# Turning 32x32 blocks on VectorE and through HBM instead of 128x128 tiles on TensorE, in a sketched-attention and token-mixing kernel

## The chip, the cores and the metric

The kernel runs on one core of a Trainium2 chip. A core has five engines that work through queues of their own and wait for each other by semaphores: TensorE (PE in the profile, with its weight loads as PEld), VectorE (DVE), ScalarE (ACT), GpSimd (POOL) and SyncE (SP, which here only issues transfers). The metric is the device time of one execution in microseconds, lower is better.

## The reference

For four batches of 1088 tokens, polynomial attention with four heads of 32 columns and features of 8 x 8, and a token mixer on its output, all in float32:

```python
def phi(x):                                   # x: (4, 4 heads, 1088, 32)
    a = einsum('rd,bhsd->bhsr', S1, x)        # r = 8
    b = einsum('rd,bhsd->bhsr', S2, x)
    return einsum('bhsi,bhsj->bhsij', a, b).reshape(..., 64)
kv  = einsum('bhsf,bhsd->bhfd', phi(k), v)
z   = phi(k).sum(axis=2)
num = einsum('bhsf,bhfd->bhsd', phi(q), kv)
den = einsum('bhsf,bhf->bhs', phi(q), z)[..., None] + 1e-06
x   = (num / den) as (4, 1088, 128)

theta = x @ w_theta
y = einsum('ts,bsd->btd', w_tok_r, x * cos(theta)) + einsum('ts,bsd->btd', w_tok_i, x * sin(theta))
u = x + y
out = u + max(u @ w_ch, 0)
```

## The kernel before

Tokens are cut into 9 chunks of 128 and handled in 3 groups of 3 chunks. The kernel does not call the engines in the order of its text: every step is recorded as an operation with its engine, its buffers and its predecessors (`op`, `buf`), and at the end the operations are issued in the order of the long string `ORDER`, with the buffer of each tile taken from the string `PLACES`. Both strings were found ahead of time by an annealing search with a planned duration for each operation (the second argument of `op`, and `fly` for a transfer). `SPINS` names operations ahead of which TensorE does some products of an idle tile. Each engine works through its own operations in this order, so an instruction that has to wait holds up all that stand behind it on its engine.

Stages, by batch `b` and group `g`:

- `load`: k, q, v by SP; `row`: the 17 rows of the token weights, 128 x 1088 in 64 bits each, loaded by SP and made into float32 by two ScalarE and two VectorE instructions a row (L564, L566, and L305 and L301 on VectorE).
- `kT`, `kf`, `kv`, `sums`, `rest`, `chain`, `kvb`: features of k, their products with v and the scales of the denominator; chains of small VectorE instructions. Batches 2 and 3 share one chain.
- `qT`, `q0`, `levels`, `den`: q turned and cut into two parts (in batches 2 and 3 the second part comes from an accumulating transfer of the POOL queue), its features by products on TensorE, and the denominators by ten VectorE instructions of a batch.
- `num` (`outputs_x`, L995): for each group VectorE makes the products of q's features, 128 tokens x 768 (3 chunks x 4 heads x 64). TensorE turns them in six 128x128 tiles (`trs`, L1019: two times three, against the identity) into two banks, ScalarE copies each bank to the tile `qT` (L1023), and two products with `bd` (k's features times v) give x, turned, which ScalarE copies to `xT` (L1032).
- `theta`: x times w_theta on TensorE; x itself turned back to tokens by three 128x128 turns (`turn`, L1052) into a bank; cosine and sine on ScalarE; VectorE multiplies the turned x with both into `z`. In batch 3, x is first scaled by a power of two (`xs`, L1044).
- `mix` for batches 0 and 1: the 17 weight rows, each times z of the batch, 512-column banks summed up over the rows; batch 0 goes through all three groups of a row at a time. Batches 2 and 3 are mixed together by seven products of half size (`winograd`), for which VectorE makes sums of weight rows (`ac`) and differences of z (`zc`).
- `out`: the last product with w_ch. The result lies turned; VectorE turns 32x32 blocks (`V.transpose`, L1161), and four stores (two on SP, two on ScalarE's queue for batches 2 and 3), one for each 32 columns, put the blocks where they belong, in runs of 32 numbers.

So a 128x128 turn on TensorE is one matmul against the identity and needs a copy out of its bank, while a VectorE turn stays within 32x32 blocks and leaves it to a transfer to put the blocks in order.

Of the kernel before, what the change touches and what calls it, by code (L numbers as in the profile page):

```python
# [29 lines left out]
    "6 4 2 5 44 0 1 47 342 3 45 7 50 8 347 49 9 10 11 58 12 29 48 13 76 83 14 46 70 64 15 84 86 16 133 87 77 85 71 "  # L30
    "26 17 139 146 30 89 88 19 72 140 78 73 343 147 74 90 21 18 149 134 27 345 79 91 94 25 150 20 40 80 92 65 32 93 "
    "31 344 41 95 99 127 148 100 43 66 157 151 337 135 22 102 158 101 67 96 128 303 42 68 103 97 348 311 35 28 104 "
    "313 105 36 304 159 305 106 315 160 350 136 108 307 161 306 107 137 109 308 59 23 129 110 314 309 24 111 316 "
    "237 61 112 312 195 33 113 98 130 231 37 238 114 225 115 131 232 152 244 34 69 116 310 233 60 239 226 75 117 "
    "196 123 118 38 81 349 119 120 122 121 346 422 234 357 240 82 424 338 351 53 352 426 425 317 423 153 340 427 "
    "339 428 154 39 429 382 62 124 155 430 141 208 156 125 431 245 201 162 432 126 189 202 197 163 190 433 165 164 "
    "198 318 358 166 191 227 63 434 209 142 359 167 203 435 132 168 436 138 228 367 204 192 169 56 437 171 170 372 "
    "354 438 172 362 143 439 441 173 452 442 174 144 440 353 175 443 51 210 176 445 453 145 444 455 178 446 177 246 "
    "456 179 448 360 447 459 449 180 341 460 461 450 454 181 462 457 182 186 463 183 185 187 184 451 361 521 464 "
    "465 519 355 522 458 466 523 520 356 467 524 468 469 484 525 369 526 527 368 485 470 528 471 377 473 188 57 529 "  # L40
    "472 486 364 530 474 220 531 487 532 363 533 221 374 534 488 392 535 373 542 538 536 549 539 543 537 545 211 "
    "544 550 212 552 546 540 553 247 551 222 215 547 541 213 365 554 548 214 248 475 555 366 556 251 572 558 477 "
    "557 559 574 489 370 560 478 561 575 479 371 564 562 480 476 216 566 563 54 481 252 567 217 249 568 199 569 581 "
    "250 378 483 604 482 605 576 375 570 565 582 218 571 577 606 379 376 573 607 578 387 583 384 579 584 580 253 "
    "393 193 235 223 194 254 224 219 394 255 261 200 265 383 262 608 397 266 205 609 268 267 264 380 585 263 610 "
    "385 206 395 269 323 207 270 389 396 611 586 324 271 321 381 319 587 320 273 588 388 272 274 241 627 322 628 "
    "275 407 390 276 490 412 229 398 831 629 386 277 589 278 399 400 279 630 631 401 402 408 590 612 280 281 632 "
    "297 391 491 835 414 832 492 409 283 410 282 413 411 417 493 403 284 415 291 404 405 494 325 406 495 292 416 "
    "419 496 285 326 286 418 833 327 287 288 290 497 420 293 421 498 289 296 52 834 294 499 500 654 501 507 652 655 "
    "508 650 653 502 298 651 633 256 656 328 634 657 513 332 299 591 658 514 635 659 257 592 660 330 661 636 662 "  # L50
    "593 258 594 55 663 259 331 595 664 333 637 665 596 666 597 673 503 598 329 638 674 334 676 669 335 667 504 639 "
    "677 336 295 505 675 230 300 236 599 668 242 670 680 678 260 243 671 679 681 672 640 688 613 687 683 641 689 "
    "684 695 690 614 691 693 714 692 682 712 694 715 697 716 713 698 301 717 685 699 718 600 686 719 515 720 703 "
    "601 696 705 721 642 700 789 302 701 706 790 516 707 704 702 791 709 780 708 722 615 781 723 616 724 711 808 "
    "517 792 710 518 809 725 617 618 726 619 506 727 810 742 643 620 735 743 728 745 782 744 793 746 838 644 736 "
    "749 621 783 737 738 622 731 729 784 645 730 747 732 739 733 740 734 811 741 798 748 799 750 800 762 751 753 "
    "764 801 765 755 785 752 756 794 766 757 623 768 754 624 758 771 836 812 773 802 759 774 813 770 760 803 761 "
    "795 775 828 763 776 772 767 848 839 777 769 840 841 837 849 778 804 829 850 860 786 851 779 842 886 843 862 "
    "787 852 857 926 830 625 646 788 853 861 796 854 858 868 855 844 856 845 859 864 814 869 797 805 863 877 865 "
    "846 647 878 889 879 870 927 871 887 904 847 880 890 881 930 872 866 806 602 894 867 882 603 883 888 873 928 "  # L60
    "874 967 815 626 807 875 932 905 884 934 509 876 895 892 818 648 896 931 906 933 907 939 929 897 937 940 891 "
    "816 885 941 510 908 935 948 909 936 949 893 898 950 938 924 819 942 910 911 943 951 899 912 952 913 944 925 "
    "953 817 945 820 954 822 821 946 900 649 947 901 968 902 955 903 970 956 957 511 980 958 512 823 971 824 981 "
    "825 982 972 983 826 919 984 920 973 969 974 959 990 961 991 975 921 976 922 923 914 992 960 915 977 916 978 "
    "917 962 979 985 964 963 827 1000 986 918 1001 987 993 965 994 988 1002 966 995 989 996 1004 997 1003 998 1005 "
    "1006 999 1007 1010 1008 1011 1012 1009 1013 1014 "
)
PLACES = (
    "3 1 9 1 1 11 1 21 2 13 15 7 1 9 1 16 6 19 4 0 5 6 0 3 6 3 4 4 1 1 11 3 2 5 6 8 2 1 0 2 4 6 5 2 2 0 7 8 0 1 7 3 "
    "5 5 2 9 6 1 0 4 6 5 7 4 2 1 12 1 7 4 2 0 0 2 0 1 8 4 4 4 3 19 2 5 4 6 14 0 6 0 5 1 7 4 11 1 2 7 8 0 0 7 1 7 21 "  # L70
    "4 0 3 3 7 5 6 1 2 2 6 3 10 12 3 2 2 3 5 8 14 3 4 4 1 4 1 2 2 0 0 6 3 2 2 9 10 5 0 4 0 0 5 21 7 10 7 6 11 3 6 1 "
    "3 0 7 7 11 1 6 4 7 2 6 7 9 5 1 0 4 4 6 7 2 3 7 0 0 2 6 5 3 0 2 3 2 0 12 2 6 8 3 11 10 0 7 18 3 17 5 1 20 17 3 "
    "16 0 4 9 11 3 2 13 2 9 15 3 19 20 1 4 1 1 9 16 1 9 2 3 9 19 2 4 4 3 9 0 7 1 2 11 4 6 0 0 3 5 3 6 0 4 3 4 4 2 2 "
    "5 2 5 6 7 3 3 1 2 7 0 3 6 5 4 3 3 0 2 2 3 5 3 1 0 4 3 2 5 9 7 4 0 4 7 0 2 2 1 2 1 1 3 0 0 7 7 1 3 2 7 2 0 7 7 "
    "4 1 4 1 3 2 3 5 0 0 5 0 1 0 6 3 7 14 6 6 0 3 1 6 5 3 4 3 1 7 1 0 2 4 7 6 1 3 0 6 5 4 5 4 2 0 6 3 4 21 1 21 1 4 "
    "2 5 2 6 2 3 6 4 4 1 1 6 5 0 4 4 3 1 0 0 4 0 6 6 0 1 7 1 4 5 7 14 2 3 0 4 6 2 5 0 2 3 2 6 4 5 4 2 1 6 3 3 2 4 7 "
    "1 5 "
)
SPINS = (
    "76:2 139:4 158:1 109:1 166:1 172:5 174:1 1010:1 "  # L80
# [15 lines left out]
QDMA = (False, False, True, True)  # L96
UDMA = (True, True, False, False)
# [124 lines left out]
def dve2(n):  # L222
    return (n / 2 + 150) / 960.0
# [11 lines left out]
def kernel(  # L235
# [49 lines left out]
    pools = {c: maker(c, w) for c, (_, w) in classes.items()}  # L285
    L = Layout(classes)
# [30 lines left out]
    def vop(n, fn, w, r, two=False, lk=0):  # L317
        op("V", dve2(n) if two else dve(n), fn, w, r, lk=1 if two else lk)

# [675 lines left out]
    def outputs_x(b, lv, pool_qp):  # L995
# [3 lines left out]
        for g in range(NG):  # L999
# [13 lines left out]
            qT = buf("g3", (2, GW), F32, "qT")  # L1013
            for n in range(2):
                tr = buf("ps", (GW,), F32, "qptr")

                def trs(n=n, tr=tr, qp=qp):
                    for i in range(GC):
                        T.transpose(tr()[:, i * P:(i + 1) * P],  # L1019
                                    qp()[:, i * H + 2 * n:i * H + 2 * n + 2].rearrange("p h i j -> p (h i j)"), ident())  # L1020

                op("P", 0.33, trs, [tr], [qp])
                op("A", act(GW), lambda n=n, tr=tr, qT=qT: A.copy(qT()[:, n], tr()), [(qT, n)], [tr])  # L1023
            xp = buf("ps", (GW,), F32, "xp")

            def num(xp=xp, qT=qT):
                for n in range(2):
                    mm(xp()[n * 64:(n + 1) * 64], bd()[:, 2 * n:2 * n + 2].rearrange("p h d -> p (h d)"), qT()[:, n],
                       True, True)
# [7 lines left out]
        for g in range(NG):  # L1037
            at("theta", b, "_", g)
            x = buf("ps", (GC, P), F32, "x")
# [10 lines left out]
            def turn(x=x, xs=xs, off=off):  # L1050
                for i in range(GC):
                    T.transpose(x()[:, i], xs()[:, off + i * P:off + (i + 1) * P], ident())  # L1052

            def theta(g=g, th=th):
                for i in range(GC):
                    y_ = xt()[:, g * GW + i * P:g * GW + (i + 1) * P]
                    mm(th()[:, i], y_, w2()[:, 0], True, True)

            op("P", 0.67, theta, [th], cells(xt, g * GW, (g + 1) * GW) + [w2])
            op("P", 0.33, turn, [x], dep)  # L1060
            op("A", act(GW), lambda cs=cs, th=th: A.activation(cs()[:, 0], th(), AF.Copy, bias=ROUND), [(cs, 0)], [th])  # L1061
            vop(GW, lambda cs=cs, th=th: stt(cs()[:, 1], cs()[:, 0], ROUND, th(), ALU.subtract, ALU.subtract), [(cs, 1)],
                [th, (cs, 0)])
# [303 lines left out]
```

## Time and profile before

| | |
|---|---|
| three runs | 222.06, 221.21, 222.2 us, median 222.06 |
| the profiled execution | 222.07 us, its span 220.3 us |
| granted TensorE clock | 0.997 |
| VectorE busy | 173.8 us (79%) in 395 instructions |
| ScalarE busy | 117.0 us (53%) in 228 |
| transfers | 23195 packets, 34.68 MB; 17028 of them under 512 bytes |

Each group line of the profile reads: line, engine, operation, out<-in by the program's names, partitions x elements, count | busy us in all, mean ns of one | idle time just before, and what ended it. Most helpers record all their operations in one line (L301 for two-operand VectorE work, L321 for TensorE products), so lines are told apart by tiles and shapes. Busy times of neighbours on an engine overlap a little, since the next instruction starts before the one ahead has drained; the time from start to start is shorter than the busy time.

### The profile page before, as it was taken

How to read it: one execution, taken by the hardware profiler on the slowest of the kernel's cores; microseconds unless marked ns; L12 is line 12 of the kernel's file. 1: busy time of each engine (PE TensorE's matmuls, PEld its weight loads, DVE VectorE, ACT ScalarE, POOL GpSimd, SP SyncE). 2: the span in 40 equal slices, each digit the busy share in tenths (PEclk: the TensorE clock that was granted, in tenths of full speed). 3: DMA queues.
4: the chain of work that ended last, by engine and by line, in shares of the span. 5: the costliest groups of instructions: out<-in, count | busy, mean ns of one | idle time of the engine just before them, and what ended most of it. 6: DMA issues, size and time to landing. Idle time of an engine off the chain costs nothing.

```text
span 220.3 us, 5088 instructions
## 1 busy us (share of the span) xinstructions
PE 213.3 (97%) x2052; PEld 160.9 (73%) x2052; DVE 173.8 (79%) x395; ACT 117.0 (53%) x228; POOL 22.6 (10%) x44
## 2 busy tenths in 40 slices
PE   7999998999999999999999999999999999999993
PEld 3787897776678576766667668777688888788872
DVE  4699999999989998998906862899268899955661
ACT  3799998789978985675324355633484000000000
POOL 2356000000050110000222040000200000000000
PEclk9999999999999999999999999999999999999998
DMA  5999099993979863775435342003400002102373
GB/s 166 413 417 402 22 332 391 360 413 86 343 228 244 221 240 152 288 318 204 98 119 88 122 110 39 1 11 54 68 0 0 3 0 46 26 0 43 53 102 76
DMA packets 23195, 34.68 MB, mean 157 GB/s; under 512 B 17028, under 2 KB 18308, under 8 KB 20996
## 3 DMA queue, kind: packets, MB, share of 16 engines
q1 hardware_dynamic: 17908, 29.28, 37.9%
q0 software_dynamic: 1728, 4.65, 9.9%
q10 hardware_dynamic: 3536, 0.43, 1.3%
q8 instruction: 16, 0.26, 0.5%
q14 instruction: 7, 0.06, 0.1%
HBM read 27.48 MB, written 2.23 MB: 135 GB/s over the span
## 4 chain that ended last, share of the span: by engine, by line
PE 85%; DVE 8%; ACT 2%; issue 2%; DMA 1%; POOL 1%; POOLq 0%
PE ps L321 75%; PE ps L1019 4%; PE ps L359 3%; DVE big L301 2%; PE ps L1052 2%; DVE g L301 1%; PE ps L927 1%; DMA out<-g 1%; DVE lv L301 1%; PE ps L703 1%; DVE hf L305 1%; DVE sm L308 1%; ACT big L614 1%; ACT g L706 1%; DVE big L305 0%
## 5 line engine op out<-in xcount | busy, mean ns | idle before, releaser
L321 PE MATMUL ps<-big,zs 128*128 128x384 f32 (+4 forms) x398 | 111.6, 423 | 0.4 <-DVE big L301 0.4
L321 PEld LDWEIGHTS ps<-big,zs 128*128 128x128 f32 x398 | 71.2, 190 | 26.7 <-issue 0.8
L1151 ACT COPY g<-ps 128x128 f32<-128x128 f32 (+1 forms) x3 | 0.9, 301 | 48.1 <-PE ps L1143 47.8
L566 ACT ACTIVATE big<-zs 128x1088 int32<-128x1088 uint32 (+1 forms) x18 | 21.1, 1177 | 4.9 <-DVE big L301 3.2
L301 DVE CUSTOM_DVE_ANT_0 big<-big,big 128x2176 uint16<-128x2176 uint16 x17 | 21.8, 1285 | 0.4 <-ACT big L566 0.4
L321 PE MATMUL ps<-big,big 128*64 128x64 f32 (+2 forms) x208 | 21.7, 276 | 0.0
L564 ACT ACTIVATE big<-zs 128x1088 f32<-128x1088 f32 x17 | 20.7, 1217 | 0.8 <-DMA zs<-w_tok 0.7
L321 PEld LDWEIGHTS ps<-big,big 128*64 128x64 f32 (+1 forms) x208 | 16.7, 154 | 3.0 <-issue 0.5
L301 DVE TENSOR_TENSOR big<-big,big 128x544 f32<-128x544 f32 x24 | 16.7, 716 | 0.1
L1023 ACT COPY g<-ps 128x384 f32<-128x384 f32 x24 | 10.4, 485 | 11.1 <-PE ps L1019 10.1
L301 DVE TENSOR_TENSOR zs<-ps,g 128x768 f32<-128x768 f32 (+2 forms) x20 | 12.5, 629 | 2.9 <-ACT g L1065 2.6
L315 POOL DMA_DIRECT2D big<-hf x6 | 5.9, 986 | 81.6 <-DVE sm L305 40.3
L305 DVE TENSOR_SCALAR big<-big 128x1088 int32<-128x1088 int32 x17 | 12.2, 721 | 0.6 <-ACT big L564 0.6
L301 DVE TENSOR_TENSOR g<-lv 128x768 f32<-128x768 f32 x12 | 11.0, 954 | 0.6 <-PE ps L321 0.5
L321 PEld LDWEIGHTS ps<-w,big 128*128 128x128 f32 x80 | 10.3, 192 | 1.6 <-issue 0.6
L308 DVE SCALAR_TENSOR_TENSOR g<-g,ps 128x384 f32<-128x384 f32 x12 | 6.5, 550 | 5.9 <-ACT g L1061 5.7
L321 PE MATMUL ps<-w,big 128*128 128x128 f32 x80 | 11.1, 277 | 0.0
L1019 PEld LDWEIGHTS ps<-ident,g 128*128 128x128 f32 x72 | 8.2, 141 | 2.3 <-issue 0.8
L1061 ACT ACTIVATE g<-ps 128x384 f32<-128x384 f32 x12 | 5.7, 490 | 7.9 <-PE ps L321 5.3
L359 PE MATMUL ps<-idle 128*128 128x384 bf16 x27 | 8.0, 414 | 1.9 <-POOL idle L361 1.3
L1019 PE MATMUL ps<-ident,g 128*128 128x128 f32 x72 | 9.5, 275 | 0.0
L308 DVE SCALAR_TENSOR_TENSOR big<-ps,even,big 128x256 f32<-128x256 f32 (+1 forms) x10 | 4.8, 497 | 5.7 <-PE ps L321 5.7
(185 smaller groups left out, 339.6 us busy)
## 6 DMA issues: line engine op xcount, KB each, us to landing
zs<-w_tok SPq DMA_DIRECT2D x17, 1088.0 KB, 7.0
big<-k_l SPq DMA_DIRECT2D x6, 576.0 KB, 6.0
big<-hf POOLq DMA_DIRECT2D x6, 576.0 KB, 5.1
big<-q_l SPq DMA_DIRECT2D x4, 576.0 KB, 9.4
big<-v_l SPq DMA_DIRECT2D x4, 576.0 KB, 10.8
g<-big POOLq DMA_DIRECT2D x4, 192.0 KB, 3.8
out<-g SPq DMA_DIRECT2D x16, 48.0 KB, 1.9
g<-big POOLq DMA_DIRECT2D x2, 160.0 KB, 3.2
```

The source lines that it names most:

```text
L301: eng.tensor_tensor(out=o, in0=a, in1=b, op=f)
L305: (eng or V).tensor_scalar(out=o, in0=a, scalar1=s1, scalar2=s2, op0=op0, **kw)
L308: (eng or V).scalar_tensor_tensor(out=o, in0=a, scalar=s, in1=b, op0=op0, op1=op1)
L315: op("G", 0.9, lambda: G.dma_start(dst(), src(), accum_op=ALU.add), w, r, fly=fly)
L321: T.matmul(o, lhs, rhs, start=start, stop=stop, skip_group_check=True)
L359: T.matmul(nowhere() if home is None else view(home, (GW,), F32), idle()[:, 0:P], idle(), start=True, stop=True, skip_group_check=True)
L564: op("A", 0.22 + n * 0.0009, lambda: A.activation(dfn(), words_of(raw(), n)[1].bitcast(F32), AF.Prelu, scale=2.0**-112, alpha=-(2.0**32)), ...
L566: op("A", 0.22 + n * 0.0009, lambda: A.activation(stp(), words_of(raw(), n)[0].bitcast(U32), AF.Copy, scale=2.0**-29), [stp], [raw])
L1019: T.transpose(tr()[:, i * P:(i + 1) * P], qp()[:, i * H + 2 * n:i * H + 2 * n + 2].rearrange("p h i j -> p (h i j)"), ident())
L1023: op("A", act(GW), lambda n=n, tr=tr, qT=qT: A.copy(qT()[:, n], tr()), [(qT, n)], [tr])
L1052: T.transpose(x()[:, i], xs()[:, off + i * P:off + (i + 1) * P], ident())
L1061: op("A", act(GW), lambda cs=cs, th=th: A.activation(cs()[:, 0], th(), AF.Copy, bias=ROUND), [(cs, 0)], [th])
```

## The change

Two lists, `NFAR` and `XFAR`, say for which batches a turn is made in the new way: the products of q's features of batches 2 and 3, and x of batch 2. In these, a new helper `turned` records three operations in place of TensorE's turns: one VectorE transpose of all 32x32 blocks (768 columns for a group of q, 384 for one of x), four writes to a scratch tensor in HBM, one for each 32 partitions, that put the blocks at their turned places in runs of 32 numbers, and one plain read back into the tile. The writes and the read are on SP's queue, and the read waits until the four writes have landed. For q this replaces six TensorE turns and two ScalarE copies; for x it replaces three turns, and the tile `x` now lies in the memory on the chip rather than in a bank. The product `num` reads its operand by chunk with a step, because the two head pairs lie side by side. The order, the buffers and the idle products (`SPINS`) were searched for anew, starting from the order before.

```diff
-    "6 4 2 5 44 0 1 47 342 3 45 7 50 8 347 49 9 10 11 58 12 29 48 13 76 83 14 46 70 64 15 84 86 16 133 87 77 85 71 "
+    "6 4 2 5 44 0 1 45 58 3 47 7 50 8 342 48 11 9 46 12 347 13 76 83 14 49 64 337 15 77 84 86 65 10 87 16 29 94 17 "
...
 SPINS = (
-    "76:2 139:4 158:1 109:1 166:1 172:5 174:1 1010:1 "
+    "76:2 15:2 84:2 89:6 135:1 189:1 166:3 439:2 521:1 1005:1 "
 )
...
+NFAR = (False, False, True, True)
+XFAR = (False, False, True, False)
...
+    far = ctx.enter_context(tc.tile_pool(name="far", bufs=1, space=bass.MemoryType.DRAM))
...
+    def turned(cls, dst, src, r, n, name):
+        blocks = buf(cls, (n,), F32, "tb")
+        vop(n, lambda: V.transpose(out=blocks(), in_=src()), [blocks], r)
+        there = Buf(None, (n,), F32, name)
+        there.ap = far.tile([P, n], F32, tag=name, name=name)
+        nf = P // SQ
+
+        def scatter():
+            for f in range(nf):
+                SY.dma_start(there().rearrange("(a i) (x b j) -> b i x a j", a=nf, b=nf, j=SQ)[f],
+                             blocks()[f * SQ:(f + 1) * SQ].rearrange("i (x a j) -> i x a j", a=nf, j=SQ))
+
+        op("S", 0.0, scatter, [there], [blocks], lk=nf, fly=1.8, n=n * nf)
+        op("S", 0.1, lambda: SY.dma_start(dst(), there()), [dst], [there], lk=1, fly=4.6)
...
+            if NFAR[b]:
+                qT = buf("g3", (GC * 2 * P,), F32, "qT")
+                turned("g3", qT, lambda qp=qp: qp().rearrange("p n i j -> p (n i j)"), [qp], GC * 2 * P, f"fq{b}{g}")
+                qTn = lambda n, qT=qT: qT().rearrange("p (c n t) -> p n c t", n=2, t=P)[:, n]
+            else:
...
+                qTn = lambda n, qT=qT: qT()[:, n].rearrange("p (c t) -> p c t", t=P)
...
-                    mm(xp()[n * 64:(n + 1) * 64], bd()[:, 2 * n:2 * n + 2].rearrange("p h d -> p (h d)"), qT()[:, n],
-                       True, True)
+                    mm(xp()[n * 64:(n + 1) * 64].rearrange("m (c t) -> m c t", t=P),
+                       bd()[:, 2 * n:2 * n + 2].rearrange("p h d -> p (h d)"), qTn(n), True, True)
...
-            x = buf("ps", (GC, P), F32, "x")
+            x = buf("g1", (GC * P,), F32, "x") if XFAR[b] else buf("ps", (GC * P,), F32, "x")
...
-            op("P", 0.33, turn, [x], dep)
+            if XFAR[b]:
+                turned("g1", x, lambda xs=xs, off=off: xs()[:, off:off + GW], dep, GW, f"fx{b}{g}")
+            else:
+                op("P", 0.33, turn, [x], dep)
```

## The prediction

> **What bounds the kernel now.** I read the page first, then the chain of waits in order of time, the windows, the groups by shape and the transfers. A span of 220.3 us lies in an execution of 222.07 us; the median of the three runs shown is 222.06 us, so sums made against this execution hold for the median as they stand. A change under 0.5% (1.1 us) can't be told from none.
>
> The first two parts of the page and the chain in order of time (start, length, what):
>
> ```profile
> PE 213.3 (97%) x2052; PEld 160.9 (73%) x2052; DVE 173.8 (79%) x395; ACT 117.0 (53%) x228; POOL 22.6 (10%) x44
> ```
>
> ```profile
> 34.88 0.34 PE ps L359
> ...
> 66.23 0.33 PE ps L1052 x3
> ...
> 126.87 1.31 PE ps L1019 x12
> ...
> 216.84 0.29 DVE g L308
> ```
>
> From 34.88 us to the last product the chain is TensorE's own queue, one instruction behind the other. A turn there costs 0.33/3 or 1.31/12, both 0.109 us. But "TensorE is the bound" is only half of it. The windows (busy time and count of PE, PEld, DVE, ACT, POOL; clock; DMA share; GB/s):
>
> ```profile
> 35.00:60.00 25.00, 24.96 (x309) 18.14 (x309) 24.66 (x56) 22.52 (x39) 0.00 (x0) 1.00 0.81 310
> 60.00:85.00 25.00, 24.88 (x313) 17.65 (x312) 22.91 (x45) 20.08 (x41) 4.48 (x5) 1.00 0.82 246
> 85.00:110.00 25.00, 25.00 (x93) 16.16 (x92) 23.60 (x48) 15.04 (x17) 1.29 (x1) 1.00 0.56 200
> 110.00:130.00 20.00, 20.00 (x235) 14.28 (x235) 11.14 (x25) 7.92 (x17) 4.10 (x6) 1.00 0.38 94
> 130.00:150.00 20.00, 20.00 (x181) 14.78 (x178) 12.68 (x26) 9.59 (x22) 0.77 (x2) 1.00 0.23 47
> ```
>
> Up to 110 us VectorE is as full as TensorE (24.66 of 25, 22.91, 23.60); after it, it is little over half full. A shorter TensorE queue pays only where VectorE can deliver sooner.
>
> **What leaves and what comes.** The groups by shape (busy us, mean ns | idle before):
>
> ```profile
> L1019 PE MATMUL ps<-ident,g 128*128 128x128 f32 x72 | 9.5, 275 | 0.0
> ...
> L1023 ACT COPY g<-ps 128x384 f32<-128x384 f32 x24 | 10.4, 485 | 11.1 <-PE ps L1019 10.1 <-ACT g L1023 0.8 <-PE ps L321 0.2
> ...
> L1161 DVE STREAM_TRANSPOSE g<-g 128x384 f32<-128x384 f32 x4 | 2.3, 572 | 0.0
> ...
> L1161 DVE STREAM_TRANSPOSE g<-big 128x256 f32<-128x256 f32 x2 | 0.9, 445 | 1.4 <-DMA out<-g 1.4
> ```
>
> TensorE loses half of the 72 turns of q (batches 2 and 3: 36) and the 9 turns of x of batch 2: 45 x 0.109 = 4.9 us, all from the chain. ScalarE loses 12 of 24 copies (12 x 0.485 = 5.8 us), after 110 us, where it is under half full: nothing. Five more idle products (32 for 27, 0.18 us each by the chain's five in 0.92 us) stand nearly all ahead of 35 us, where TensorE waits: nothing, 0.9 us if all were on the path. VectorE gains six turns of 768 columns, which no row shows. From 256 to 384 columns the rows rise by 127 ns, 0.99 ns a column, so 768 cost 0.572 + 384 x 0.00099 = 0.95 us; bounds are two of 384 (1.14) and the 128x768 product of VectorE (0.95). Three of 384 columns come on top. Consecutive VectorE instructions overlap by about 0.09 us, so start to start it is 6 x 0.87 + 3 x 0.48 = 6.7 us more. The product with x reads the same number of columns from the same number of rows, from on-chip memory rather than TensorE's banks; the row 128x768 costs 0.954 us either way (g<-lv and zs<-ps,g).
>
> **The HBM trip.** Transfers (KB each, median us to landing):
>
> ```profile
> q10 hardware_dynamic: 3536, 0.43, 1.3%
> ...
> out<-g SPq DMA_DIRECT2D x16, 48.0 KB, 1.9
> ```
>
> 1.3% of 16 engines' 220.3 us over 3536 packets is 13 ns for a packet of at most 128 bytes. A trip of q writes 3072 such packets: 3072 x 13 / 16 = 2.5 us of all engines, spread over four issues that the store rows show 0.48 us apart. So: issues 1.9, landing of the last 1.9 (stores: 1.5 to 3.3), read issue 0.35. No row has a 384 KB read on a free queue; the nearest is the 576 KB v load issued at 122.20, whose packets ran from 123.17 to 125.63, 3.4 us. I take 3.0, between the 2.7 of the 128 KB store and 3.4; crowded q loads took up to 11.7. A trip costs about 7.1 us for q and, with half the bytes, 6.4 for x.
>
> The built order shows what covers it. I walked each engine's new order and added start-to-start times of the rows. From the end of the first turn of x to the product that needs it, VectorE has 9.5 us of other work (the rest of batch 3's denominators, q products, one weight sum), and TensorE needs that product 0.6 us later. For q of batch 2 the cover is 13.9 us, for batch 3 some 15. All 45 new issues stand behind the last weight load and the last v load in SP's queue, so no load waits for them; one group's output store waits behind a read, which no one waits for. SP does hold later writes behind a read that waits for its own write: the reads of q of batch 3 stand behind all three writes, which leaves about 3 us of their 15. On POOL's queue the accumulating transfer of batch 3's q shares the engines with the trips: VectorE releases it 10.3 us before TensorE needs it, against 1.0 us of issue, 4.2 of landing and 3.5 of a trip's engine time (2.5 for the writes, 1.0 for the read at the v load's 188 ns a packet). The trips cost nothing, then; without the cover each would cost its 7.1 us.
>
> [...]
>
> **The new bound.** Here the order matters. Work up to the same places, start to start, in us:
>
> ```
> place (what TensorE waits for)          before: PE  DVE  trace DVE/PE    after: PE  DVE
> levels of batch 1 (chain of batch 1)           38.7 42.0  46.4 / 46.6          37.7 42.0
> first product with weight row 6                79.5 64.0  69.5 / 88.8          64.7 70.8
> k times v of batch 2                           69.6 72.5  78.4 / 78.7          68.8 73.8
> first product with weight row 16              102.8 100.2 108.8 / 112.1        91.0 96.0
> ```
>
> Before, VectorE had 8.7 us of idle time by row 16 (108.8 less 100.2) and TensorE 9.3; VectorE was 2.6 us of work ahead there. After, it is 5.0 us behind: the anneal puts row 16 11.8 us earlier in TensorE's work but only 4.2 earlier in VectorE's. So at row 16 VectorE sets the time: 96.0 plus its idle time. Bounds: 4.4 (what it had by 46.4 us, if it never waits again) and 8.7 (all of before's). A VectorE that is later waits less for others, but it waits in order and ScalarE's releases come close too; I take the middle, 6.5. TensorE then passes row 16 at 96.0 + 6.5 + 0.2 (semaphore, from the 46.4/46.6) = 102.7. Left are 201.2 - 91.0 = 110.2 us of its work (total 201.2, was 206.1) and the 1.2 us that it lost after row 16 before (10.5 at the end less 9.3): 214.1, against 216.6 before. The tail of one copy, one addition and one store is the same. Sum: -4.9 from the turns, +2.4 from the new waits, -2.5 us: 219.6 us. Behind row 16 the leads are smaller than before (the Winograd product that waits for the first difference of z: VectorE 21.7 us of work ahead before, 14.1 after), yet the waits that VectorE must make for batch 2's and 3's levels and for the last group of q leave this about even with TensorE; I hold 1 us for it in the range.
>
> **Rivals.** *TensorE alone is the bound:* VectorE waits at most 4.4 us by row 16. The full fill of 35 to 60 us speaks for it, the growing idle time of VectorE after 60 us against. 222.07 - 4.9 + 0.3 = 217.5 us.
> *VectorE waits as before* (8.7 us by row 16): TensorE ends at 216.3, 221.8 us, no change to be measured. For it: VectorE's waits after 60 us were for ScalarE and TensorE, and ScalarE's queue stays full there (22.52 and 20.08 of 25).
> *The trip is late:* the product with x sits in VectorE's order, and what is queued behind it are all further z, their sums and TensorE's next products. Beyond 9.5 + 0.6 = 10.1 us each us of the x trip is one on the path. With the slow ends of the rows (issues of 1.97, landing 3.3, a crowded read of 11.7) a trip is 23 us; at 14.0 us the x trip alone costs 3.9, 223.5 us, slower. It decides from 10.1 + 2.5 = 12.6 us. Against it: the DMA share is 0.18 to 0.38 after 110 us.
> [...]
> *It doesn't do what it says:* the built program has 140 turns on TensorE for 185, so this is out.
>
> **How the numbers follow.** Forecast 0.50 (its own range 218.6 to 220.9), TensorE alone 0.14, waits as before 0.17, trip late 0.17, a nineteenth 0.02. The first two lie below 220.95 but for 0.02: faster 0.62. Waits as before and that 0.02 are no change, 0.19, of which I move 0.02 to slower for the 1 us held above: 0.17. Slower 0.21. The range runs from 217.3 (the bound of 4.4 with a little less of the late loss) to 223.5 (the late trip's price).
>
> **What would show it.** Right: TensorE's turns at the q line fall to 36; VectorE busy about 180.5 us; around TensorE's row 16 waits for VectorE of 2 us or more in sum that before hasn't; the reads of q land 6 to 8 us after the turn, and VectorE does not wait for a transfer of x. Wrong: VectorE or TensorE waiting for these reads; TensorE without any wait between 45 and 105 us; a row 16 passed later than 105 us.

## The result, and the profile after

| | before | after |
|---|---|---|
| median of 20 runs each | 221.53 us (220.96 to 222.2) | 220.38 us (219.67 to 224.38) |
| profiled execution, its span | 222.07, 220.3 us | 219.88, 218.1 us |

Two of the 20 executions after took 224.3 and 224.38 us; medians from here on leave out executions more than 1.5% above the fastest of their kernel, which makes 220.14 us here, and below drops one execution each of dve_less (353 us), row2_less and spin_11 and two of old_all. The ratio is 0.9949 with a 95% interval of 0.993 to 0.9968: half a per cent faster, 1.4 us between the medians 221.53 and 220.14. The two profiled executions lie 2.2 us apart, because the one of before is 0.5 above its median and the one of after 0.3 below: what is read off the two traces overstates the gain by 0.8 us.

The busy times of the page after:

```profile
PE 209.8 (96%) x2012; PEld 155.3 (71%) x2012; DVE 179.1 (82%) x404; ACT 112.0 (51%) x216; POOL 22.8 (10%) x44
```

From start to start, TensorE's work fell from 205.8 to 200.9 us: the 4.9 us of the 45 turns, as forecast. VectorE has 5.3 us more, ScalarE 5.0 less, and the transfers have twice the packets (48108 for 23195). The span fell by 2.2 us only, so 2.7 us of the 4.9 came back as time in which TensorE does not work at its pace. The windows after (busy time and count of PE, PEld, DVE, ACT, POOL; clock; DMA share; GB/s):

```profile
35.00:60.00 25.00, 24.44 (x360) 18.08 (x359) 24.67 (x61) 24.07 (x45) 6.10 (x5) 1.00 0.88 292
60.00:85.00 25.00, 25.00 (x266) 17.36 (x265) 24.78 (x46) 23.18 (x44) 0.00 (x0) 1.00 0.73 271
85.00:110.00 25.00, 25.00 (x244) 17.20 (x243) 21.13 (x44) 14.97 (x21) 3.01 (x4) 1.00 0.67 215
```

VectorE is full up to 85 us, then no longer: between 85 and 110 us it has more room than before (21.13 busy against 23.60). TensorE reads 25.00 of 25 from 60 us on, which hides what follows: a busy share counts an instruction from its start to its modelled end, and small gaps between starts vanish under the overlaps (in the stretches from 59.81 and 62.38 us below, a product of 128 columns is counted as 275 to 283 ns long, the mean of its group, and takes 0.11 to 0.13 us from start to start).

The chain of waits after, where it passes from VectorE to TensorE for good:

```profile
39.67 0.88 DVE g L304
...
40.60 0.87 PE ps L1042 x6
...
113.75 53.09 PE ps L339 x302
```

Up to 40.5 us the chain runs through VectorE (denominators of batch 0, then the first product of q's features at 39.67); from there on it is TensorE, one instruction behind the other. Before, it passed to TensorE at 34.88 us.

To see where 2.7 us went, take for each TensorE instruction its start less all of TensorE's own work ahead of it (start-to-start times; idle products count as no work). This number is what the queue has lost so far. It is an estimate: it rests on one rate for each form of product, and with other averages for these rates the last line changes by some 0.4 us.

```
place in TensorE's queue            before    after   change
levels of batch 1 (about 47 us)       7.9       9.0     +1.1
first product with weight row 16      9.2      10.6     +1.4
last product                         10.5      13.1     +2.6
```

So 1.1 us is lost by 47 us, 0.3 between there and row 16, and 1.2 behind row 16. But the two executions did not start alike. Two runs below, old_x and old_all, keep the order of before and issue the same TensorE instructions up to 126 us. First before, then old_x, at the first turns of k and at the levels of batch 1:

```profile
5.54 1.96 PE L703 MATMUL ps<-ident,big 128*128 128x128 f32 x9
...
46.57 0.55 PE L321 MATMUL ps<-mv,hf 128*64 128x96 f16 x18
```

```profile
5.42 1.20 PE L719 MATMUL ps<-ident,big 128*128 128x128 f32 x9
...
45.83 0.55 PE L337 MATMUL ps<-mv,hf 128*64 128x96 f16 x18
```

In the profiled execution of before these turns took 0.21 us each from start to start, in old_x, old_all and after 0.12 to 0.13, and TensorE is 0.74 us (old_all: 0.82) later from there on. Against a start like that of after, the new order loses about 1.9 us by 47 us and not 1.1, and some 3.4 us in all, which fits the medians: 4.9 of turns less 1.4 of gain is 3.5.

Ahead of the levels of batch 1 the new order puts 1.0 us less TensorE work, but just as much VectorE work (42.0 us), and TensorE reaches the place at 46.76 us against 46.57, or 45.83 with the quicker start: there the chain through VectorE sets the time, and TensorE only waits longer. Behind row 16 there is hardly a wait; 22 steps of 0.08 to 0.15 us add up to 2.2 us, against 11 steps and 1.1 us before (both traces have one more of 0.54 us, a late wait for VectorE). A stretch ahead of row 16 shows in both timelines what such steps are (start, length, form, count). First before, then after:

```profile
59.81 2.13 PE L1019 MATMUL ps<-ident,g 128*128 128x128 f32 x18
61.87 2.16 PE L321 MATMUL ps<-g,sm 128*64 128x384 f32 x12
63.96 2.27 PE L321 MATMUL ps<-w,big 128*128 128x128 f32 x18
66.07 0.49 PE L1052 MATMUL ps<-ident,big 128*128 128x128 f32 x3
```

```profile
62.38 1.66 PE L1042 MATMUL ps<-ident,g 128*128 128x128 f32 x12
63.98 0.87 PE L339 MATMUL ps<-g,sm 128*64 128x384 f32 x4
64.78 0.87 PE L1042 MATMUL ps<-ident,g 128*128 128x128 f32 x6
65.49 0.87 PE L339 MATMUL ps<-w,big 128*128 128x128 f32 x6
66.20 0.49 PE L945 MATMUL ps<-ident,big 128*128 128x128 f32 x3
```

Before, 18 turns take 2.06 us to the next start, 12 products 2.09 and 18 products 2.11. At these rates the 18 turns, 4 products and 6 products of the second stretch would take 2.06 + 0.70 + 0.70 = 3.46 us; they take 66.20 - 62.38 = 3.82. Some 0.2 of the 0.36 us stand where one form gives way to another: the new order mixes operations in shorter runs, and here the changes cost. The rest stands inside the first twelve turns and is waiting that the profile does not count as idle time. At the seventh turn it is for VectorE, whose second product of this line it needs:

```profile
61.20 1.81 DVE L304 TENSOR_TENSOR g<-lv 128x768 f32<-128x768 f32 x2
```

This product ends at 63.01, and the seventh turn starts at 63.16. In seven of the eight traces of the changed kernel and its variants compared here it starts 0.15 us behind that end (in dve_less 0.18). In control the wait is longer, and the twelve turns take 1.74 us to the next start, not 1.60:

```profile
62.64 1.81 PE L1042 MATMUL ps<-ident,g 128*128 128x128 f32 x12
64.38 0.87 PE L339 MATMUL ps<-g,sm 128*64 128x384 f32 x4
```

Do the trips cost anything? Who waited for q's scratch tiles (engine, tile, line: us, times), then for x's:

```profile
  POOL g L318: 18.0, 1
  DVE g L325: 0.4, 1
  PEld ps L339: 0.2, 1
```

```profile
  DVE zs L304: 0.6, 1
```

TensorE's weight loads wait 0.2 us for q, VectorE 0.4 for q's writes and 0.6 for x, over all nine trips. The 18 us are GpSimd's, and stand unchanged in the run with the plain write below, whose time is the same.

### The profile page after: what moved, and what is told of

It is laid out like the page before. It is cut to its first block, busy times and chain, and to the rows that moved or that the text cites. A ratio compares the mean times of both kernels' runs of the same rounds, so it can differ in the third digit from the quotient of the medians.

```text
span 218.1 us, 5091 instructions
## 1 busy us (share of the span) xinstructions
PE 209.8 (96%) x2012; PEld 155.3 (71%) x2012; DVE 179.1 (82%) x404; ACT 112.0 (51%) x216; POOL 22.8 (10%) x44
## 2 busy tenths in 40 slices
DMA packets 48108, 40.59 MB, mean 186 GB/s; under 512 B 40789, under 2 KB 42453, under 8 KB 45909
## 4 chain that ended last, share of the span: by engine, by line
PE 85%; DVE 10%; DMA 2%; issue 1%; ACT 0%; SPq 0%; ACTq 0%; DVEq 0%
PE ps L339 77%; PE ps L1042 2%; DVE big L304 2%; DMA big<-k_l 2%; DVE g L304 2%; PE ps L1076 2%; PE ps L945 1%; DVE lv L304 1%; PE ps L377 1%; PE ps L721 1%; DVE sm L311 1%; DVE big L308 1%; DVE hf L308 1%; DVE sm L304 1%; SPq L392 0%
## 5 line engine op out<-in xcount | busy, mean ns | idle before, releaser
L339 PE MATMUL ps<-big,big 128*64 128x64 f32 (+2 forms) x208 | 20.9, 275 | 0.0
L980 ACT COPY lv<-ps 128x480 f32<-128x480 f32 x12 | 6.6, 565 | 16.1 <-PE ps L339 16.1
L339 PEld LDWEIGHTS ps<-w,big 128*128 128x128 f32 x80 | 10.8, 192 | 1.2
L339 PE MATMUL ps<-g,sm 128*64 128x384 f32 x48 | 10.0, 502 | 0.0
L377 PE MATMUL ps<-idle 128*128 128x384 bf16 x32 | 8.7, 387 | 1.3 <-POOL idle L379 1.3
L318 POOL DMA_DIRECT2D g<-big x6 | 5.2, 923 | 44.8 <-ACT g L1157 26.8
L339 PEld LDWEIGHTS <-hf 128*64 128x64 f16 (+1 forms) x288 | 7.4, 110 | 3.2 <-issue 1.9
L304 DVE TENSOR_TENSOR zs<-ps,g 128x768 f32<-128x768 f32 (+2 forms) x15 | 9.4, 627 | 0.0
```

Of the source, the lines that this page charges most:

```text
L304: eng.tensor_tensor(out=o, in0=a, in1=b, op=f)
L318: op("G", 0.9, lambda: G.dma_start(dst(), src(), accum_op=ALU.add), w, r, fly=fly)
L339: T.matmul(o, lhs, rhs, start=start, stop=stop, skip_group_check=True)
L377: T.matmul(nowhere() if home is None else view(home, (GW,), F32), idle()[:, 0:P], idle(), start=True, stop=True, skip_group_check=True)
L980: op("A", act(480), lambda g=g, lp=lp: A.copy(lv().rearrange("p l (c n) -> p l c n", n=HR)[:, :, g * GC:(g + 1) * GC], lp().rearrange("p c ...
```

## The experiments

Times are medians; the kernel before had 221.46, 221.39 and 221.47 us beside the three sets of runs. Where the changed kernel ran unchanged:

> The changed kernel itself, once more, as the reference for the kernels beside it and for another profile. Theory 1 (VectorE sets the time up to weight row 16, TensorE alone after it): 0.5% below the kernel before, about 220.4 us, and in the new profile TensorE again takes the first product with weight row 6 and with row 16 within 0.3 us of VectorE's last instruction for that row. Rival (the trips through HBM are late in part of the executions): the new profile shows TensorE or VectorE waiting for a read from the scratch tensor, and the times scatter by more than 1 us.

> The changed kernel once more, beside the two others of this set: 220.1 us (219.7 to 220.7), 0.994 of the kernel before, by every theory.

Measured: 220.13 us (ratio 0.9938, interval 0.9919 to 0.9957) and 220.11 us (0.9931, 0.9913 to 0.995). The gain beside these sets is 1.35 us. This is the base for all that follows.

**Is the strided write late?** The four writes became one plain write:

```diff
-            for f in range(nf):
-                SY.dma_start(there().rearrange("(a i) (x b j) -> b i x a j", a=nf, b=nf, j=SQ)[f],
-                             blocks()[f * SQ:(f + 1) * SQ].rearrange("i (x a j) -> i x a j", a=nf, j=SQ))
+            SY.dma_start(there(), blocks())
```

> The changed kernel with each trip's four strided writes replaced by one plain write of the same bytes, so the blocks stay where VectorE left them: one issue and 128 packets for 4 issues and 3072 (q) or 1536 (x). Theory 1 (trips covered by other work): within 0.4 us of the changed kernel. Rival (trips late, or their small packets crowd the transfers of the same time): 0.7 us or more below it, with less scatter.

Measured: 219.99 us (0.9922, 0.9899 to 0.9944). One issue of 0.32 us stands in place of four of 0.66, the first read is issued 2.9 us sooner (122.31 for 125.22 at its end), no one waits for a read of x any more, and the time is that of the changed kernel. The trips are covered.

**What is the order worth, and what the turns?** Three runs put turns back into the new order (undo_all all 45, undo_x2 those of x alone, undo_q3 those of q of batch 3 alone), two put the trips into the old one. The two lists, in this order of runs:

```diff
-NFAR = (False, False, True, True)
-XFAR = (False, False, True, False)
+NFAR = (False, False, False, False)
+XFAR = (False, False, False, False)
...
+NFAR = (False, False, True, True)
+XFAR = (False, False, False, False)
...
+NFAR = (False, False, True, False)
+XFAR = (False, False, True, False)
```

> The changed kernel's order and idle products, but all 45 turns back on TensorE (put some 2 to 3 us of TensorE work ahead of their use), no trips and no VectorE turns. All these turns stand behind weight row 16. Theory 1: TensorE's queue is the bound there, so the full 4.9 us come back: 4.0 to 4.9 us above the changed kernel, which is 2.9 to 3.8 us above the kernel before; the difference to the kernel before is what the new order lost ahead of row 16. Rival (the new order is as good as the old one, the missing gain lies in the trips): no slower than the kernel before, about 1.1 us above the changed kernel.

> The changed kernel with the nine turns of x of batch 2 back on TensorE (three operations of three turns; their VectorE turns, writes and reads are gone), q still through HBM. Theory 1 (TensorE's queue sets the end, the trips of x are covered): putting all 45 turns back cost 6.2 us, 0.138 us a turn, of which 0.109 is the turn itself; nine cost between 9 x 0.109 = 1.0 and 9 x 0.138 = 1.2 us: 221.1 to 221.4 us beside 220.1 for the changed kernel. Theory 2 (the product with x waits for the trip, and with it what is queued behind it on VectorE): without the trip that wait goes, and the time is no more than 220.3.

> The changed kernel with the 18 turns of q of batch 3 and their six ScalarE copies back on TensorE and ScalarE, batch 2 as changed. Theory 1 (TensorE's queue sets the end, VectorE and ScalarE have time left behind 130 us): 18 x 0.109 = 2.0 to 18 x 0.138 = 2.5 us more than the changed kernel, 222.1 to 222.6 us. Theory 2 (VectorE's three turns of 768 columns and the reads that stand behind all three writes in SP's queue are themselves late for the products of batch 3): less than 1.2 us more, 221.3 at most.

Measured: undo_all 226.34 us (1.0218, 1.0195 to 1.0241), undo_x2 221.77 (1.0019, 0.9998 to 1.004), undo_q3 223.3 (1.0082, 1.0069 to 1.0095): 6.2, 1.65 and 3.2 us more than the changed kernel, for turns of 4.9, 1.0 and 2.0 us. Each costs more than its turns. TensorE's loss by place says where:

```
                                   control  undo_all  undo_x2  undo_q3
levels of batch 1                    9.2      9.2       8.9     10.1
row 16                              11.0     10.7      10.6     11.7
last product                        13.4     14.3      13.6     14.8
between row 16 and the end           2.3      3.5       3.0      3.1
```

Behind row 16, where the turns are, the loss is 0.7 to 1.2 us more than in the changed kernel. For q these are waits for what a turn on TensorE brings with it, the copy out of its bank. In undo_all:

```profile
128.82 0.57 PE L337 MATMUL ps<-mv,hf 128*64 128x96 f16 x18 [0.62 <-ACT g L1044]
```

In brackets stands TensorE's idle time and what ended it: the ScalarE copies of q's turned tiles (L1044 there). In undo_q3 the like is 0.24 us at 162.93. In undo_x2 the 0.7 us are one step at 211.8, near the end, 0.45 us of it idle time that a ScalarE copy of the output ends, and not at the turns. In undo_q3 the profiled execution also came 0.9 us late to the levels of batch 1, well ahead of the edit, and its first turns of k took 1.43 us and not 0.88; what of its 3.2 us this is in the other executions stays open. The first theory holds with its sign and place, its upper ends (4.9, 1.2 and 2.5 us more) were too low.

The new order alone, undo_all against before, is 4.9 us slower than the old one. It pays only with the turns gone. And the other corner, with the order, the buffers and the idle products of before:

```diff
+NFAR = (False, False, True, True) * 4
+XFAR = (False, False, True, False) * 4
...
+NFAR = (False, False, False, False) * 4
+XFAR = (False, False, True, False) * 4
```

> The order, the buffers and the idle products of the kernel before, with all 45 turns taken off TensorE: each VectorE turn stands in VectorE's order close behind what it turns, its four writes and its read stand at the same place in SP's queue. In the trace of before the products of q of batches 2 and 3 are ready only 3.5 to 7 us ahead of the TensorE product that uses them turned, and x 4.5 us ahead of VectorE's product; a trip measured on a free queue takes 8.0 us for q and 7.2 for x, and the reads hold the next trip's writes back. Theory 1 (it is the new order that buys the cover): TensorE saves 4.9 us and waits for the trips, some 9 us in batch 2's q, 3 at x, 12 to 18 in batch 3's q: 230 to 250 us. Theory 2 (TensorE and VectorE have other work ready and the trips hide in any order): 221.5 - 4.9 = 216.6, at most 219.

> The order of the kernel before with the nine turns of x of batch 2 alone taken off TensorE, q as before. Theory 1 (a trip of 7.2 us against the 4.5 us that the old order leaves between x and VectorE's product with it, the three trips one behind the other in SP's queue): VectorE waits 2 to 8 us at these products, TensorE saves 1.0: 223 to 228 us. Theory 2 (the trip hides behind cosine, sine and the weight sums): 221.5 - 1.0 = 220.5 us.

Measured: old_all 257.25 us (1.1626, 1.1602 to 1.165) and old_x 229.06 (1.0342, 1.0329 to 1.0355). The direction is that of the first theory, and both lie above its range. The views of old_x first: VectorE's waits, TensorE's timeline and the windows:

```profile
DVE zs L302 <- DMA g<-fx: 9.5, 2, 8.8
```

```profile
145.51 1.65 PE L337 MATMUL ps<-w,big 128*128 128x128 f32 x6 [5.37 <-ACT big L1054]
```

```profile
140.00:150.00 10.00, 4.63 (x14) 3.40 (x14) 6.28 (x12) 2.94 (x7) 0.00 (x0) 0.75 0.21 42
150.00:160.00 10.00, 10.00 (x40) 7.22 (x39) 8.97 (x18) 1.70 (x5) 0.00 (x0) 0.91 0.30 57
```

VectorE waits 9.5 us for two reads of x, what is queued behind the product with x is late, and TensorE stands idle for 5.37 us. Then the granted clock is down: six products of a form that take 0.83 us elsewhere take 1.65. The kernel lost 7.7 us on the whole and saved 1.0 us of turns, so 8.7 us are to be explained: 5.4 of TensorE standing, and 3.3 left. The reduced pace behind the wait accounts for them: from 145.5 us to 151.7, where full pace comes back, TensorE's products take 3.2 us more from start to start than the same forms elsewhere. In old_all the same, three times over for q (engine, line, what it waited for: us, times, longest; then the windows and the timeline):

```profile
PE ps L337 <- DMA g<-fq: 32.6, 3, 13.8
```

```profile
180.00:190.00 10.00, 1.19 (x4) 0.59 (x6) 0.00 (x0) 0.00 (x0) 0.00 (x0) 0.50 0.51 118
```

```profile
141.56 2.83 PE L337 MATMUL ps<-g,sm 128*64 128x384 f32 x8 [13.82 <-DMA g<-fq]
```

In old_all the clock is 0.66 between 130 and 150 us and 0.50 between 180 and 190, and the eight products behind the wait of 13.82 us take 2.83 us, where eight of this form take 1.51 in undo_q3 (at 159.89). How long the fall lasts: in old_x full pace came back 6.2 us after TensorE resumed (granted 0.56 from 150 to 152 us, 1.00 from 152 on). And in the profiled execution of row2_less, a variant below (224.5 us), the clock is down 3.6 us behind a wait of only 1.66 us, which TensorE makes for ScalarE:

```profile
40.39 1.33 PE L339 MATMUL ps<-sm,pbd 128*128 128x64 f32 x6 [1.66 <-ACT sm L810]
```

```profile
44.00:46.00 2.00, 2.00 (x24) 1.67 (x24) 2.00 (x6) 0.85 (x3) 0.00 (x0) 0.50 1.00 409
```

In old_all a wait of 1.85 us, up to 155.45, left the clock at 1.00 (150 to 170 us). What decides between the two is not shown.

So the four corners are: old order with turns on TensorE 221.4, old order with trips 257.25, new order with turns 226.3, new order with trips 220.1. Neither part gains anything alone. In the two bad corners the operations were put in by hand, without a new search; and no run searched anew for an order with all turns on TensorE, so what part of the 1.4 us such a search would have found by itself stays open.

**Does VectorE set the time up to row 16?** This was the prediction's account. First VectorE's shift of weight rows 0, 3 and 8 was taken out, then, in the same manner, shift and addition of row 2:

```diff
-        op("V", n * 0.00053 + 0.15, lambda: ts(dfn().bitcast(I32), dfn().bitcast(I32), 3, ALU.logical_shift_left),
-           [dst], [], lk=1)
+        op("V", n * 0.00053 + 0.15, lambda: None if dst.name in ("w0", "w3", "w8") else
+           ts(dfn().bitcast(I32), dfn().bitcast(I32), 3, ALU.logical_shift_left), [dst], [], lk=1)
```

> The changed kernel without VectorE's integer shift for weight rows 0, 3 and 8, that is 3 instructions of 0.64 us (start to start) ahead of row 16; the weights of these rows are then wrong. Theory 1 (VectorE is the bound up to row 16): 1.2 to 1.9 us below the changed kernel, less than the full 1.9 because TensorE already stood 9.0 us behind its own work at the levels of batch 1, ahead of these rows. Rival (TensorE alone is the bound from 47 us on): no difference beyond 0.3 us.

> The changed kernel without VectorE's shift and addition for weight row 2, so that row stays at what ScalarE wrote: 0.64 + 1.20 us from start to start that stand in VectorE's order ahead of the denominators of batch 0 and of all that follows. Theory 1 (the first 47 us are a chain through VectorE, ScalarE and TensorE in turn; ScalarE's copy of the levels of batch 0 ends at 30.84, 0.42 us ahead of the VectorE instruction that takes it, so at most 0.4 us can be had): 219.7 us, the levels of batch 1 on TensorE no more than 0.5 us earlier. Theory 2 (VectorE's own work sets the first 47 us): 1.8 us less, 218.3 us.

Measured: dve_less 219.8 us (0.9929, 0.9909 to 0.9949), row2_less 219.95 (0.9947, 0.9923 to 0.997). About 2 us less of VectorE's work, ahead of or on the way to row 16, buys 0.15 to 0.35 us, hardly more than these runs tell from nothing. In dve_less VectorE spends most of that time waiting for ScalarE, where in after none of its waits between 44 and 103 us is over 0.12 us:

```profile
48.13 2.49 DVE L304 CUSTOM_DVE_ANT_0 big<-big,big 128x2176 uint16<-128x2176 uint16 x2 [0.55 <-ACT big L584]
...
76.41 0.96 DVE L304 TENSOR_TENSOR zs<-ps,g 128x768 f32<-128x768 f32 x1 [0.44 <-ACT g L1092]
```

So VectorE alone is not the bound: with less of its work ScalarE and TensorE are right behind. For the first 47 us row2_less says so by its time alone. VectorE still holds TensorE up a little, at the turns of 63 us above. The timelines of after at row 16, VectorE's addition first, then TensorE:

```profile
100.06 1.28 DVE L304 CUSTOM_DVE_ANT_0 big<-big,big 128x2176 uint16<-128x2176 uint16 x1
```

```profile
99.77 3.82 PE L339 MATMUL ps<-big,zs 128*128 128x384 f32 x12
```

Row 16 is ready at 101.34 us and used from 101.59 on, but the twelve products around it, eight of 384 columns and four of 320, run without a gap: 12 x 0.305 from start to start on average and 0.16 for the end of the last are 3.82. The same 0.25 us stand in again (101.92 and 102.17), as its expectation wanted, but in dve_less too (102.28 and 102.53), with three shifts less: they are no wait at this place.

**What makes executions of one kernel differ?** At the start TensorE does idle products, then the first turns of k.

```diff
-    op("P", 1.73, lambda: [spin() for _ in range(10)], [nowhere], [idle])
+    op("P", 1.73, lambda: [spin() for _ in range(11)], [nowhere], [idle])
```

> The changed kernel with 11 instead of 10 idle products at the start of TensorE's queue. In the traces of the changed kernel and its variants the first six turns of k take 0.87 us in some executions and 1.4 to 1.5 in others, and the place of the levels of batch 1 comes 0.5 to 1.0 us later in the latter; TensorE stands idle for 0.40 to 0.45 us ahead of these turns. Theory 1 (full pace comes sooner without that gap): the turns take 0.87 us each time and the median falls by 0.3 to 0.5 us, 219.6 to 219.8. Theory 2 (the moment at which full pace comes has nothing to do with the gap): 220.1 to 220.3, with the same spread.

Measured: 220.09 us (0.9947, 0.9927 to 0.9966), no change: the second theory. The first instructions of spin_11, then of the changed kernel beside it:

```profile
5.05 0.84 PE L377 MATMUL ps<-idle 128*128 128x384 bf16 x2
5.69 1.48 PE L721 MATMUL ps<-ident,big 128*128 128x128 f32 x6
```

```profile
5.47 0.88 PE L721 MATMUL ps<-ident,big 128*128 128x128 f32 x6
```

In spin_11 there is no gap ahead of the turns of k, and they still take 1.48 us, 0.21 us a turn from start to start, about half the pace of the 0.109 us elsewhere; in the other execution they take 0.88 us, 0.12 a turn. Both executions start TensorE at 1.34 us. That this is drawn anew in each execution fits the traces (the loss at the levels of batch 1 is 8.9 to 9.4 us where these turns take 0.9 us and 9.8 to 10.4 where they take 1.4 to 1.5, over nine traces; in the profile of before, too, they took 0.21 us a turn). The granted clock from 5.5 to 7.5 us reads 1.00 in before, with its slow turns, and in after alike, so it does not show the cause; what draws it was not tried.

## Why the prediction came out as it did

Forecast 219.6 us, 2.5 us faster; measured 220.14, 1.4 us faster. The direction and the range hold; how near the sum comes to the trace is in part luck, as the fifth point shows.

- *The turns, 4.9 us off TensorE:* right (205.8 to 200.9 us of its own work).
- *ScalarE's copies worth nothing:* the 5.0 us of busy time were not on the path after 110 us. But undo_all and undo_q3 show that turns on TensorE bring waits of 0.2 to 0.6 us for these copies in this order, 0.9 us in all in undo_all, so their absence is worth something here.
- *The turn of 768 columns, 0.95 us:* 0.98 us in the trace. VectorE busy 179.1 against the 180.5 forecast.
- *The trips cost nothing:* right. The terms were small: four issues took 2.8 us and not 1.9 (0.66 us each), and a trip of q alone in the queue, the last in old_all, took from 180.58 to 188.7, 8.1 us and not 7.1. Behind each other's writes it took 12.0 in the changed kernel (116.46 to the read's landing), near the 13.9 of cover. The sign "reads land 6 to 8 us after the turn" was missed: the six reads were issued 6.4 to 10.7 us after it and landed 3.5 to 5.4 us later where the trace has the landing. The rival of a late trip is thereby out for this order; the old order shows its price. The prediction charged only the lateness itself (3.9 us for a trip of x of 14.0 us) and not the pace that TensorE loses behind a wait (3.2 us behind the 5.37 us in old_x).
- *At row 16 VectorE sets the time, +2.4 us:* this is the step that failed. TensorE passes row 16 at 101.59 and not 102.7, VectorE had lost 5.35 us by then and not 6.5, and TensorE had nearly all of its 10.6 us already at weight row 4 (71 us). Between the two traces 2.6 us came back, nearly the size of the term, for other reasons: 1.1 us at the chain up to the levels of batch 1, 0.3 up to row 16, 1.2 in small steps behind it. That the last product starts at 214.1 us, as summed, is luck: 1.1 us less by row 16 and 1.3 us more behind it cancel. The prediction had carried before's 7.9 us of early loss over unchanged, and priced TensorE's work by rates from long runs of one form.
- *The rival "TensorE alone is the bound", 217.5 us:* its mechanism is the nearer one from 40 us on, but for the wait at 63 us; its time is 2.6 us too low, since it charged 0.3 us for all that came back.
- *A nineteenth for the strided write, a chance of 0.02:* no run shows such a factor. The writes of q (96 KB each, in runs of 128 bytes) landed in 2.9 us at the median in the changed kernel, and with one plain write in place of four the time is the same (219.99 us against 220.13).
- *The base:* the forecast subtracted 2.5 us from an execution of 222.07 us as if it were the median; over 20 runs the median is 221.53. From there the same sum gives 219.0, 1.1 us under the 220.14 measured: the base was too high by 0.5 and the gain by 1.1, and the one covered part of the other. Between medians 4.9 - 1.4 = 3.5 us came back and not 2.6; 0.74 to 0.82 of the difference is the slow start of the profiled execution of before, as old_x and old_all show.

No version that beats the changed kernel came out of the runs; plain_write, dve_less and row2_less leave work out and lie within 0.35 us of it.

## What to carry to other kernels

A saving on the engine that sets the end is worth its full price only where the engine's order stays as good (here 4.9 us of turns gave 1.4): compare the queue's loss by place (start less own work ahead), not busy shares, and charge for shorter runs of one operation (some 0.2 us between 62.38 and 66.20 us here). Moving work from a full engine through memory needs an order with cover for the whole trip, queue included (8.1 to 12.0 us for q here); without it, the same edit that gains 1.4 us here loses 36: TensorE waited 32.6 us for the reads of q in old_all, and its granted clock fell too, to 0.75 in the window around a wait of 5.4 us (old_x) and 0.66 around one of 13.8 us (old_all). A trace in which an engine shows no idle time can still hold short waits, as at TensorE's seventh turn at 63.16 us: compare starts over several traces. Make the sum against a median of many runs, or say how far the profiled execution lies from it and where: here 0.75 us of it lay in the first 8 us.

## What the runs showed of the hardware

- In the changed kernel an issue of a write in 128-byte runs took 0.57 to 2.06 us, 0.66 at the median for the 768 packets of q; in plain_write the plain write of four times the bytes took 0.32 in one issue.
- In old_x TensorE waited 5.4 us. Its granted clock was 0.75 from 140 to 150 us and 0.91 from 150 to 160, six products behind the wait took 1.65 us for 0.83 elsewhere, and full pace came 6.2 us after the wait. In row2_less the clock was 0.50 from 44 to 46 us, 3.6 us behind a wait of 1.66 us; in old_all it stayed at 1.00 behind one of 1.85 us.
- The first six turns of k took 0.88 us in control and 1.43 in undo_q3, with the same TensorE instructions ahead of them; with an eleventh idle product at the start (spin_11) they took 1.48, and the median was the same (220.09 against 220.11).
